# The same instructions of an attention and expert kernel, listed in another order

## The chip, the cores and the metric

One core of a Trainium2 chip runs the whole program. The metric is the device time in microseconds (us) of one execution, the median of three. The engines are PE (TensorE), DVE (VectorE), ACT (ScalarE), POOL (GpSimd) and SP (SyncE); SP computes nothing here and issues nearly all DMA transfers, one after the other.

## What is computed

Four batches of 12,608 tokens with 128 channels go through attention over 49 agents, and then 128 tokens of each batch, those with the largest score, through a small expert network.

```python
scale = 1.0 / np.sqrt(q.shape[-1])
agent_v = sm(agents, k) @ v          # softmax over the tokens, per agent
x = sm(q, agents) @ agent_v          # softmax over the agents, per token
scores = x @ w_gate
top_idx = argpartition(-scores[b], capacity)[:capacity]      # capacity 128
ye = relu(x[b, top_idx] @ w1) @ w2                           # 128 -> 1024 -> 128
out[b, top_idx] = x[b, top_idx] + sigmoid(scores[b, top_idx])[:, None] * ye
```

## The kernel before

Each batch's tokens are cut into seven blocks, six of 15 tokens for each of 128 partitions and one of 9 (`CHUNKS`). A block of q, k or v is one DMA of 960 KB (968 with v's column of ones), or 576 KB for the short one, into one of the eight tiles of the ring `in` (N_IN = 8). Results go out in blocks of the same sizes from tiles of the same ring. So a tile of `in` holds a load until PE has read it, or results from the first eviction into it until the store has landed.

The stages of a batch are these. **Keys** (`keys`, `scores`): PE multiplies a block of k with the agents (line 339, eight matmul records in the profile for each of two halves), DVE transposes the products into a tile (345) and takes their maximum (352); when all seven blocks are in, the maximum over the batch is spread over the partitions (369 to 384, `mb`). **Values** (`values`): POOL subtracts the maximum (394), ACT takes the exponential (397), and PE multiplies with the block of v (409). All blocks of a batch add up in the one bank `v`. `values_end` scales the result into the weights `ws` (425 to 466). **Queries** (`queries`): a block of q is multiplied and transposed like k; then the largest of each token (479, DVE), subtraction (481, POOL), exponential (483, ACT); for batch 0 alone the division too (485 to 490); a split into two halves of 16 bits (493 ACT, 494 POOL); a transposition on PE (509), copied out of PSUM by ACT or DVE (512). Queries need neither keys nor values, so their blocks may come early. **Gates** (533) and **rates** (547 to 561) give each token's score and divisor. **Results** (`results`): PE multiplies the transposed queries with `ws` (579), up to four tokens in a bank; DVE or ACT evicts the bank with the scaling (587 to 595) into an `in` tile, and SP stores it (600). **Choice and expert** (`topk`, `expert`): the 128 best of a batch (613 to 687), a gather by POOL (717), the network (725 to 831), a scatter by POOL (835) into the stored result, so after its stores.

The code records all this as some 1,300 operations with what they read and write, and then issues them in the order of a table of numbers, `ORDER`: each entry is an operation's number times two, plus one where the second of two allowed engines takes it (evictions and copies may go to DVE or ACT). Nothing else sets the order: `issue` goes through the table, gives each operation its tile from the ring (the one that became free first), and puts it at the end of its engine's queue. Every engine, SP included, works through its own queue in order; an instruction that has to wait holds up all that stand behind it on that engine.

```python
for code in order:
    i, way = code >> 1, code & 1
    engines, _, fn, bufs, after = self.ops[i]
    self._take(bufs)
    fn(engines[way])
```

The batches overlap: SP loads queries of batches 0 to 2 first, then keys of 0 and 1, and so on, as the table says. PSUM has six banks for scores, transpositions and results (ring `b`), one for the values and one for the gates.

Of the kernel before, what the change touches and what calls it, by code (L numbers as in the profile page):

```python
# [103 lines left out]
ORDER = (
    "0ca0cc0cg0ce0ci0t40t60ck0cm0co0cq0cs0cu0t80cw0cy0d00ns0nu0ny0ta0nw0o00tc0te0tg0ti0tk0tm0a20a80oo0ou0ow0aa"
    "0o20o40o60oq0os0a40qg0qm0qo0ts0tv0a60ac0ae0qi0pk0pm0to0pq0b60bc0b80po0qk0qq0ps0ag0o80ai0oa0qs0be0ba0tq0rc"
    "0ri0re0rk0bg0oy0bi0p008y0940oc0900og0pu0pw0rg09609209806q09a0ak0rm0am0oe0d20d40py0bk0oi06s06w06y06u07u0ro"
    "0ao00k15c08007w0bm0700bo0bq08207y00s00m07200u15i15e0rq09c0rs0ru0740p20p408400o15k0bs00q07600w15g09e15m05m"
    "0s00rw05o0d60bu0ry0d80s20p60qu09g0bw00y05q0100pc01201401605s05u0p80by0c101a07807a05w0aq0c20pe0q00pa0as01c"
    "01k0240ji02601e01m01o01i0180jq01g0c509i01q02i0060au0ay0js02a0ju01s01y0qw0b002802k02o02m02q01w02u01u02c022"  # L110
    "05y0q207c0aw07e08607g0qy15o15q0j40s802002e07i00e02g00i00g07m00800c0sa0q809k07o09m00a02w02y0300sc0se032034"
    "09o0880360qa02s07l08a0sg04u0021680iq16a0r00q40r416e16c0si06008c0iy0is16g0r316i0j215s15u03g03q08e0iu08g0sk"
    "03a0jw0380r609u0j609w0ko03k0ka0ic15w15z06206403i09q03c03e0iw0660j00q70kq0jy0k20ku0k40k80jk0ja09s0680kw0l0"
    "0j803m03o0jc0ky0jo0ks0jg0k60jm0je0ie0kc0ki0ik0ii0io0kg0km0l20ke0k00kk03u04404e04y04o18000003s0sm04a04004c"
    "08i0so0sq0sw04203w03y04604804g0ig0sy1600l408k16k16m04k08m08q0ss0l60l804m16o04w16208o0im08t0la0lm06a06c0n0"
    "04i04q04s0500521860540su0lc0lw16q05605818218418806e06i06k05a17417617817a17c05c06g0m60le05e05i05k05g14g14m"
    "14i19s19y19u14o1a014k0ma18w0lq0m00lg0fa0ea0fs0ed0lo0fu0fk0fm14q19w08w0e60b20b40e90fd16s0f60dy0f90e10c80e2"
    "0fg14s14u16u18a0ly0e50ee17e0041a207s06m06o09y0f20f40a007q0g218y1921940mg0mq0ms16w0dc0c608u0da1901960de0fy"
    "0g40gu0fj16y14w0m817g18c1a418e17i0n20mi14y17k1a617m0fo0li0lk0ls0lu0m20m40mk0mu0mc0me0mm0mo0mw0my1qg0n40n6"
    "0n80na0gw1060g00ey18g1540f00fr18i18k18m1560ze1ns11c0nc1080ne10a10c10e0ng0ni17s17u1qi18o1qm1qo0nk0no10i1nu"  # L120
    "1nw0nm1qk0fe0z01ny10g1o017o17q1a811e1qq18r0zm11k11m1501531980nq0gk0ra0go0pi0r81qs19a1qu0gn0ty0t20gg0zo11g"
    "0zq0gi11i0gr0z20z80z60za11o0z40zc10y0t011611010k0zs0do0g60s419c0dr0ds0dv0g910m0zg1181121o21o41o611a10o10q"
    "1000zi0zk1140zu1040zy0zw10s1m00gs10w0eo10211q0ga1m61m20tw0ok1m81m41l41241mw19e1o81oa0qc0pg11s0ek0er0hg11u"
    "11w1ma11y0gd0en0ge1aa10u0qe0om1ac0dg0es0s61oc0u00ho0hu0dj0ev12u12w1ae12k1l61la1lc0xi1l81n21n41my1oe1200hq"
    "0hs1220xm19g1ag1n019j0gy0he0y20h80xk0h00ha0hw1ai0y40uq12y12e12o13412a13o1mc1qw12m0hm12c1qy13e13q0yk0hk0yg"
    "1360u20y60h40xy0xw0xu13g0yi0hi0ya0yc13812612812g12i12q12s13013213a13c13i13s0fw0h60xq0us1n60y019k19n1le0h2"
    "0hc0uu0ye0ux1me0y80xo13k13m13u13w0um0up0xs0vm1r01r20vo13y0vy0eg0ei1400uy0w10v11gu1gg1g20v21420wc0wg0we0vu"
    "0dk0wj0vw0vq0vt1440w40w71go1461gq1gs1h21gw1r41480dn14a1h60vc0ve1r714c14e1lg1n81h01g40vg1gy0vj1mg1na1nc0wu"
    "0wm15a1700w818s1g60wa1h41g81660v80ew0dw1i01fo1h80w20wk1hm1pk0vb1gi1ga1mi0ww0hy19o1gm1gc0wp0i01gk0i21ge1li"
    "1ne1mo0ug1ak0u80ub0uj0i40i60wq17w1am18u0u41720i81580wy17y1640wt1mr0ia0u60uc19q1mk1ao0v41hg1ha0x11mm1lk1aq"  # L130
    "0v70uf1e61hk1hi1fw1hc1i21fq1i81fy1i61g01i41he1nk1dw0ym1ds1nn1ia1ic0yo1fs0yq1fu1hu1ho1hy1hs1dz1dv1lm1ls1lu"
    "1og1oo1ie1hq1hw1oi1pm1ig0ys1ea1ng1ii1ik1ni1pq1eo1im1ou1oq1po0yu1ow0yw1os1ps1pu1eg0yy1ee1eq1ei1e01e21ek1ec"
    "1e81oy1em1es1io1iq1c01bw1iy1j81is1j21jc1jm0vk1j01ji1f61eu1ew1ja1ey1jk1f01js1pw1k21kc1p01iu1iw1j41j61je1jg"
    "1jo1jq1f21f41c21c41c61be1by1f81fa1fc1fe1ci1bs1bm1fg1ca1jw1k61kg1ju1wm1wk1py1ck1k41p21p41ke1q01jy1k01k81ka"
    "1ki1kk1bp1bu1fi1bg1cc1q21fk1di1dl1km1fm1ko0x81as1q81ce0xb0x21we1e41c81wc0uk1kq1au1qb1ch1wo1p61q41b01q71b3"
    "1ks1ku1kw1l01l21cw1lo1cs1p81cy1ky1de1pc0xc1ra1ly1qe1no1pb0xe1pf1lr1dh1dm1ok1cm1wq1nq1om1d41ms1ws1cu1do1wu"
    "0x41pi1mu1qc1lw1pg1r81cp1ww0x61wy1d71x01x21s61da1d01uk1s21x41dd1rc1uu1uw1re1uy1s41x61s81sa1d31un1sd1vg1x8"
    "1to1ba1ry1v61v01vc1xc1bc1wi1cq1dq1wg0xg1d81tq1s01se1vw1vu1vq1vm1vs1xm1xo1vi1vk1xa1xe1xy1xi1xq1xl1y11xt1vo"
    "1tg1ya1tk1y21v41v21va1v81ve1ti1yd1y51tn1vy1w01w21bi1ts1tu1rg1w41y61u21ss1bl1tw1bq1rj1y91w61w81wa1rs1sk1sg"
    "1b41sv1yy1u41sm1aw1sj1ay1xu1b71ro1rq1so1sq1xx1ru1t21rk1ta1tc1ty1u61rn1u81yg1z01ua1t61u11z21t41z41z61uc1yk"  # L140
    "1sy1z81za1zc1ze1ug1uo1zg1xg1t91t11zi1ui1yi1ur1zm1zs1zw1zy1zk1b81rw1sw1ue1ye1yo1yq1zu1yu2021yw1te1us1ym1zo"
    "1zq2001ys204206"
)


# [904 lines left out]
```

## Time and profile before

| | |
|---|---|
| median of three runs | 295.34 us (294.12 to 296.73) |
| the profiled execution's own time | 295.63 us |
| its span, first to last instruction | 293.6 us |
| PE, DVE, ACT, POOL busy | 262.5, 224.1, 180.5, 143.2 us |
| moved by DMA | 106.67 MB |

Busy time is the time in which an engine has an instruction at work. Overlapping matmuls are counted once, so back-to-back work and work with small holes can look alike. "[3.46 <-DMA in<-kT]" behind an instruction means that its engine was idle for 3.46 us ahead of it and that the landing of a block of k ended the wait. A line of waits reads: engine, what it waited to do, what it waited for, us in total, how often, the longest.

### The profile page before, as it was taken

Reading aid. Unit: us, or ns where it says so; the run is one execution under the profiler, and the core shown is the slowest. Engines: PE = TensorE matmul, PEld = TensorE weight load, DVE = VectorE, ACT = ScalarE, POOL = GpSimd, SP = SyncE. Lnnn points to the kernel's source line nnn. Section 1 sums busy time; section 2 is a strip of 40 time slices with the busy share of each in tenths; the row PEclk is TensorE's granted clock in tenths of the full one; section 3 lists DMA queues with packets and bytes.
Section 4 is the critical chain, followed back from the end, with each engine's and each line's share of the span. In section 5 each row is a group of like instructions: output and inputs, shape, how many; then the busy total and the mean of one; then the engine's idle time right before and its main releaser. Section 6 shows DMA issues by size and latency. Waiting matters only on the chain.

```text
span 293.6 us, 8629 instructions
## 1 busy us (share of the span) xinstructions
PE 262.5 (89%) x3524; PEld 179.6 (61%) x3524; DVE 224.1 (76%) x516; ACT 180.5 (61%) x405; POOL 143.2 (49%) x110
## 2 busy tenths in 40 slices
PE   2897989899999999998999997798599999999990
PEld 1232334245497689845476896484358889968990
DVE  1598999999973893379977996697469858998740
ACT  1243896375554799144469979387337877899340
POOL 1457987979959697201649500532019951001022
PEclk9999999999999999999999999999789999999997
DMA  7999999999999979999998999998978996696991
GB/s 270 426 425 426 422 420 419 418 419 423 416 416 414 421 307 354 366 424 395 317 422 333 421 353 343 415 279 312 360 282 262 421 421 252 247 376 284 400 400 51
DMA packets 18587, 106.67 MB, mean 363 GB/s; under 512 B 2544, under 2 KB 3824, under 8 KB 18544
## 3 DMA queue, kind: packets, MB, share of 16 engines
q1 hardware_dynamic: 17760, 105.42, 91.2%
q8 instruction: 29, 0.48, 0.6%
q0 software_dynamic: 256, 0.52, 0.5%
q10 hardware_dynamic: 528, 0.13, 0.2%
q14 instruction: 14, 0.11, 0.1%
HBM read 79.85 MB, written 26.21 MB: 361 GB/s over the span
## 4 chain that ended last, share of the span: by engine, by line
PE 45%; DMA 30%; DVE 17%; ACT 4%; issue 2%; POOL 0%; POOLq 0%; SPq 0%; DVEq 0%; ACTq 0%
PE b L339 15%; PE v L409 12%; DMA in<-qT 12%; DMA out<-in 9%; PE b L579 8%; DMA in<-va 6%; DVE s L345 6%; PE b L509 5%; DVE mx L352 3%; DVE qm L479 3%; DMA in<-kT 3%; ACT in L595 2%; ACT ga L633 2%; DMA ag_sb<-agT 1%; PE x L533 1%
## 5 line engine op out<-in xcount | busy, mean ns | idle before, releaser
L339 PE MATMUL b<-in,ag_sb 128*32 128x480 f32 (+1 forms) x896 | 99.0, 567 | 19.0 <-DMA in<-kT 6.7
L345 DVE STREAM_TRANSPOSE s<-b 128x480 f32<-128x480 f32 (+1 forms) x112 | 67.7, 630 | 13.5 <-PE b L339 12.6
L339 PEld LDWEIGHTS b<-in,ag_sb 128*32 128x32 f32 x896 | 26.0, 112 | 64.4 <-issue 28.8
L394 POOL TENSOR_TENSOR s<-s,mb 128x735 f32<-128x735 f32 (+1 forms) x28 | 46.7, 1696 | 25.0 <-DVE mb L384 25.0
L579 PE MATMUL b<-ws,s 98*128 98x128 f16 x792 | 55.6, 219 | 1.6 <-DVE in L592 1.6
L512 ACT COPY s<-b 98x1024 f16<-98x1024 f16 (+2 forms) x36 | 32.3, 920 | 33.3 <-PE b L509 33.3
L494 POOL TENSOR_TENSOR f<-s,f 128x735 f16<-128x735 f32 (+1 forms) x28 | 41.1, 1475 | 23.5 <-ACT f L493 18.7
L579 PEld LDWEIGHTS <-s 98*128 98x128 f16 x792 | 47.8, 98 | 6.8 <-issue 5.5
L481 POOL TENSOR_TENSOR s<-s,qm 128x735 f32<-128x735 f32 (+1 forms) x28 | 38.1, 1369 | 26.2 <-DVE qm L479 18.0
L409 PE MATMUL v<-in,s 128*64 128x129 f32 x792 | 47.6, 274 | 1.7 <-DMA in<-va 1.7
L595 ACT ACTIVATE in<-b,r 128x128 f32<-128x128 f32 x149 | 40.9, 386 | 12.5 <-PE b L579 7.6
L409 PEld LDWEIGHTS v<-in,s 128*64 128x64 f32 x792 | 44.3, 136 | 4.1 <-DMA in<-va 1.2
L352 DVE TENSOR_REDUCE mx<-b 128x1 f32<-128x480 f32 (+1 forms) x56 | 32.9, 608 | 7.4 <-PE b L339 7.4
L509 PEld LDWEIGHTS <-f 128*98 128x98 f16 x396 | 25.5, 126 | 21.0 <-issue 14.6
L483 ACT ACTIVATE s<-s,lift 128x735 f32<-128x735 f32 (+1 forms) x28 | 24.4, 884 | 19.2 <-POOL s L481 19.1
L509 PE MATMUL b<-idh,f 128*98 128x128 f16 x396 | 30.7, 224 | 1.7 <-POOL f L494 1.4
L592 DVE TENSOR_TENSOR in<-b,r 128x512 f32<-128x512 f32 (+2 forms) x40 | 24.8, 645 | 5.1 <-DMA out<-in 3.2
L397 ACT ACTIVATE s<-s 128x735 f32<-128x735 f32 (+1 forms) x28 | 21.9, 790 | 5.4 <-POOL s L394 5.4
L628 DVE SCALAR_TENSOR_TENSOR ge<-b,top,minus 128x512 bf16<-128x512 f32 x32 | 23.9, 748 | 1.6 <-PE b L620 0.8
L479 DVE TENSOR_REDUCE qm<-s 128x15 f32<-128x735 f32 (+1 forms) x28 | 23.6, 856 | 0.2
L493 ACT CAST f<-s 128x735 f16<-128x735 f32 (+1 forms) x28 | 22.0, 788 | 2.8 <-POOL s L490 1.6
L633 ACT ACTIVATE ga<-b,top 128x512 bf16<-128x512 f32 x32 | 22.0, 689 | 0.8 <-PE b L620 0.3
(132 smaller groups left out, 227.4 us busy)
## 6 DMA issues: line engine op xcount, KB each, us to landing
in<-va SPq DMA_DIRECT2D x24, 967.5 KB, 8.0
in<-qT SPq DMA_DIRECT2D x24, 960.0 KB, 12.2
in<-kT SPq DMA_DIRECT2D x24, 960.0 KB, 9.8
out<-in SPq DMA_DIRECT2D x24, 960.0 KB, 8.1
in<-va SPq DMA_DIRECT2D x4, 580.5 KB, 8.8
in<-qT SPq DMA_DIRECT2D x4, 576.0 KB, 5.3
in<-kT SPq DMA_DIRECT2D x4, 576.0 KB, 9.9
out<-in SPq DMA_DIRECT2D x4, 576.0 KB, 6.6
```

The costliest lines, as they stand in the source:

```text
L339: nc.tensor.matmul(ps()[32 * i:32 * i + 32, :w], ag_sb[:, b, 32 * h:32 * h + 32], x()[:, w * i:w * i + w], start=True, stop=True,)
L345: nc.vector.transpose(s()[:, :n, 32 * h:32 * h + 32], ps()[:, :w].rearrange("p (t c) -> p t c", c=32))
L352: op("V", f"M{n}", lambda _, h=h, ps=ps: nc.vector.tensor_reduce(top[:, c, h:h + 1], ps()[:, :w], axis=AX.X, op=ALU.max), r=[ps], w=[(f"mx ...
L394: op("G", f"X{n}", lambda _, sv=sv, n=n: nc.gpsimd.tensor_tensor(sv(), sv(), d["mb"].unsqueeze(1).broadcast_to([P, n, A]), op=ALU.subtract ...
L409: nc.tensor.matmul(av()[o:o + AP_, :C + 1], s()[:, t], x3[:, t], start=(j < 2), stop=(j >= COLS - 2))
L479: op("V", f"qm{n}", lambda _: nc.vector.tensor_reduce(m, sv(), axis=AX.X, op=ALU.max), r=[s], w=[f"qm{b}{c}"])
L481: op("G", f"qx{n}", lambda _: nc.gpsimd.tensor_tensor(sv(), sv(), wide, op=ALU.subtract), r=[f"qm{b}{c}"], w=[s])
L494: op("G", f"ql{n}", lambda _: nc.gpsimd.tensor_tensor(f()[:, :n, A:], sv(), f()[:, :n, :A], op=ALU.subtract), r=[s, (f, 0)], w=[(f, 1)])
L509: nc.tensor.transpose(wide_pt()[:R, P * (t - lo):P * (t - lo) + P], f()[:, t, :], idh)
L512: (nc.vector.tensor_copy if e == "V" else nc.scalar.copy)(flat(ft()).bitcast(F16)[:R, P * lo:P * hi], wide_pt()[:R, :P * (hi - lo)])
L579: nc.tensor.matmul(p3()[:, t - lo], d["tile", c](t), ws[:, b, i, :C], start=(i == 0), stop=(i == 1))
L595: nc.scalar.activation(o4[:, t - lo], p3()[:, t - lo], AF.Copy, scale=d["r"][:, j0 + t:j0 + t + 1])
```

## The change

The table `ORDER` has other entries in the same number; the diff has nothing else. The new order was found with a charge on transfers that are issued late. One line of it stands for all:

```diff
@@ -102,44 +102,44 @@
 ORDER = (
-    "0ca0cc0cg0ce0ci0t40t60ck0cm0co0cq0cs0cu0t80cw0cy0d00ns0nu0ny0ta0nw0o00tc0te0tg0ti0tk0tm0a20a80oo0ou0ow0aa"
+    "0ca0cc0ce0cg0ci0ck0cm0co0cq16816a16c0cs16e16g0cu0cw0t40t616i16k16m16o0b60bc0be0b80ba0bg0bi17417617a1780bk"
...
```

Every engine's queue moves nearly everywhere. Two places of SP's queue are shown. "in_67" is one of the eight tiles in_64 to in_71; "out" is the result in memory; the last number is the columns of a block.

The first is the place of the first store, batch 0's second block. SP's queue before:

```order
L326 DMA in_70<-va 128x1935
L326 DMA in_69<-va 128x1935
L326 DMA in_71<-va 128x1935
L600 DMA out<-in_64 128x1920
L326 DMA in_65<-va 128x1935
L326 DMA in_71<-va 128x1935
L326 DMA in_70<-qT 128x1152
```

SP's queue after the change, at the same store:

```order
L326 DMA in_65<-va 128x1935
L326 DMA in_68<-va 128x1935
L600 DMA out<-in_70 128x1920
L326 DMA in_66<-qT 128x1920
L326 DMA in_67<-kT 128x1920
L326 DMA in_71<-kT 128x1920
L326 DMA in_68<-va 128x1935
L326 DMA in_70<-va 128x1935
```

The store was SP's 49th transfer and is now the 50th; the next load into the tile that it reads stands five rows behind it.

The second place is the keys of batch 3, among the stores of batches 0 and 1. SP's queue before:

```order
L600 DMA out<-in_65 128x1920
L600 DMA out<-in_70 128x1920
L600 DMA out<-in_66 128x1920
L326 DMA in_71<-kT 128x1152
L326 DMA in_70<-kT 128x1920
L326 DMA in_66<-kT 128x1920
L600 DMA out<-in_67 128x1920
L600 DMA out<-in_64 128x1920
L326 DMA in_67<-kT 128x1920
L326 DMA in_64<-qT 128x1920
L326 DMA in_70<-qT 128x1920
```

SP's queue after the change, with the last block of batch 0 (128x1152) and the keys of batch 3:

```order
L600 DMA out<-in_68 128x1152
L326 DMA in_67<-kT 128x1920
L326 DMA in_70<-kT 128x1920
L600 DMA out<-in_71 128x1920
L326 DMA in_66<-kT 128x1920
L326 DMA in_69<-kT 128x1920
L326 DMA in_64<-kT 128x1920
L326 DMA in_67<-kT 128x1152
L326 DMA in_70<-kT 128x1920
L600 DMA out<-in_65 128x1920
L600 DMA out<-in_68 128x1920
L326 DMA in_69<-qT 128x1920
```

Before, four loads here go into a tile that a store two or three rows ahead of them empties. After, none of the loads shown does; the tile in_68 is stored twice with no load into it between.

## Rows read from the trace of the kernel before

**Rows 1.** The page, part 1: busy us, share of the span, instructions.

```profile
PE 262.5 (89%) x3524; PEld 179.6 (61%) x3524; DVE 224.1 (76%) x516; ACT 180.5 (61%) x405; POOL 143.2 (49%) x110
```

**Rows 2.** The page, parts 2 and 3: all packets, and the queue that SP feeds.

```profile
DMA packets 18587, 106.67 MB, mean 363 GB/s; under 512 B 2544, under 2 KB 3824, under 8 KB 18544
q1 hardware_dynamic: 17760, 105.42, 91.2%
```

**Rows 3.** By stage: length; PE, PEld, DVE, ACT, POOL busy; clock, DMA share, GB/s.

```profile
10.00:100.00 90.00, 83.19 (x947) 40.05 (x940) 78.92 (x149) 51.41 (x73) 73.16 (x51) 1.00 1.02 420
100.00:115.00 15.00, 15.00 (x304) 13.46 (x303) 12.19 (x18) 13.88 (x21) 10.16 (x7) 1.00 0.87 333
115.00:240.00 125.00, 113.18 (x1628) 82.14 (x1625) 92.62 (x230) 80.28 (x194) 50.63 (x36) 0.97 0.95 360
287.00:293.60 6.60, 0.00 (x0) 0.00 (x0) 0.57 (x3) 0.00 (x0) 1.00 (x2) 0.78 0.10 35
208.00:216.00 8.00, 5.06 (x34) 2.27 (x38) 3.19 (x9) 2.33 (x8) 0.00 (x0) 0.57 0.97 353
5.16:115.00 109.84, 102.41 (x1275) 54.90 (x1277) 92.69 (x169) 65.73 (x94) 84.26 (x59) 1.00 1.00 409
```

**Rows 4.** Waits of the SP queue, 94 to 240 us: total, times, longest.

```profile
SPq L326 <- DMA out<-in: 36.7, 7, 9.2
...
SPq L600 <- ACT in L589: 15.3, 2, 13.1
```

**Rows 5.** Timeline of SP's issues, 94 to 110 us: start, length, issue.

```profile
94.14 0.33 SPq L326 DMA_DIRECT2D in<-va  x1
107.62 0.35 SPq L600 DMA_DIRECT2D out<-in  x1
```

**Rows 6.** Timeline of SP's issues, 174 to 230 us.

```profile
193.28 0.86 SPq L600 DMA_DIRECT2D out<-in  x2
203.41 0.34 SPq L326 DMA_DIRECT2D in<-kT  x1
...
225.51 2.97 SPq L326 DMA_DIRECT2D in<-va  x3
```

**Rows 7.** Waits of PE, 115 to 240 us, the three longest groups.

```profile
PE b L339 <- DMA in<-kT: 6.7, 3, 3.5
PE v L409 <- DMA in<-va: 1.7, 5, 0.4
PE b L579 <- DVE in L592: 1.6, 1, 1.6
```

**Rows 8.** DMA issues at 94 and at 203 us: size, us to landing.

```profile
in<-va SPq DMA_DIRECT2D x1, 967.5 KB, 13.6
in<-kT SPq DMA_DIRECT2D x1, 960.0 KB, 7.4
```

**Rows 9.** Timeline of PE, 200 to 222 us.

```profile
210.94 3.43 PE L339 MATMUL b<-in,ag_sb 128*32 128x480 f32 x16 [3.46 <-DMA in<-kT]
...
215.80 1.01 PE L339 MATMUL b<-in,ag_sb 128*32 128x480 f32 x8
...
218.80 2.63 PE L339 MATMUL b<-in,ag_sb 128*32 128x480 f32 x24
```

**Rows 10.** Timeline of PE at 71 us and from 105 to 122 us.

```profile
71.34 3.59 PE L339 MATMUL b<-in,ag_sb 128*32 128x288 f32 x40
...
106.09 0.61 PE L579 MATMUL b<-ws,s 98*128 98x128 f16 x8
...
110.47 10.13 PE L409 MATMUL v<-in,s 128*64 128x129 f32 x180
```

**Rows 11.** The page, part 5: line, count, busy, mean ns, idle before it.

```profile
L394 POOL TENSOR_TENSOR s<-s,mb 128x735 f32<-128x735 f32 (+1 forms) x28 | 46.7, 1696 | 25.0 <-DVE mb L384 25.0
L397 ACT ACTIVATE s<-s 128x735 f32<-128x735 f32 (+1 forms) x28 | 21.9, 790 | 5.4 <-POOL s L394 5.4
```

**Rows 12.** Waits of ACT for a store to land, 100 to 290 us.

```profile
ACT in L595 <- DMA out<-in: 4.9, 1, 4.9
```

More of the change, by code (lines that the diff above doesn't have):

```diff
@@ L104 @@
 ORDER = (
-    "0ca0cc0cg0ce0ci0t40t60ck0cm0co0cq0cs0cu0t80cw0cy0d00ns0nu0ny0ta0nw0o00tc0te0tg0ti0tk0tm0a20a80oo0ou0ow0aa"
[L106 to L139, printed above, removed]
@@ L140 @@
-    "1b41sv1yy1u41sm1aw1sj1ay1xu1b71ro1rq1so1sq1xx1ru1t21rk1ta1tc1ty1u61rn1u81yg1z01ua1t61u11z21t41z41z61uc1yk"
-    "1sy1z81za1zc1ze1ug1uo1zg1xg1t91t11zi1ui1yi1ur1zm1zs1zw1zy1zk1b81rw1sw1ue1ye1yo1yq1zu1yu2021yw1te1us1ym1zo"
-    "1zq2001ys204206"
+    "0ca0cc0ce0cg0ci0ck0cm0co0cq16816a16c0cs16e16g0cu0cw0t40t616i16k16m16o0b60bc0be0b80ba0bg0bi17417617a1780bk"
+    "0bm17c16q14g14m0ta14i14k14o17e17g14q0oo0oq0ou14s14u0ow0ns0nu0ny0os0tc0nw0oy0p008y0900940920o00960980pk0pm"
+    "14w14y0p20p409a0p60qg17i0bo0pq16w0qi0o20po0ps0t80bq0te0o40tg0qk07u16s08009c08209e0pu16u09g0bs0pw0p80o616y"
@@ new lines @@
+    "0py0q00a207w07y0a40a60840a80pc0qm0aa0860pf0pa08801c01k01o01e0q205m0qo01m01g08a05s0bu0q80qa08c0qq05u0q417k"
+    "0q606q06s06w0ac08e06y0bw17m15406u05o00y1500c201005q17o15615201i09i05w0060080by01407001208g08i0ti17q0c40o8"
+    "01q00a00e0c100c00i01s01u01w17s00g0ae09k0qs0qu17u02400k02i02c0160260ag0oa0og0oi09m0rc0ji0ka0ic02e00m00s028"
+    "02a01a02g01807208k02q0oc0oe08q09o05y08m00w08o0740qw0qy00u00o00q02u01y02k02202o02w09u02y02s02m0re0r00tk030"
+    "08s0r40iq0020j402003209q03409t0r70cy09w0600620r20tm0rg0ai0to0ri0tq0ik0ki0ts04u03g0d00tu0760km0jq0iy0ie078"
@@ new lines @@
+    "0ak04w0360rk0kk03q04004k03i0380640420io0am0ao0aq0js0ii07a0ig0jc0kc0kg03a0jg0ju0j00ke03k03u0ko0jw03c03e03s"
+    "0j60je0ja0j203m0d203o0jk0is0im0kq03w03y0k404404e04o04y0000ks07c0iu0jm0j80jo0k60ku0kw0k80jy07e07g04a04c066"
+    "0k20rm0l00iw0680d60d80d404m0as0ro0rq0rs0ru0l204604804g04i07i07k04q0l407m04s0500521pk0l60ky0l80540la05607o"
+    "0k00580lc0lg1pq1pm0rw05a15c19s1l41mw0le0li0lk0ry05c05e05g05i0ga0gd0g60g91po0ea0e20e50g20dy0s00s31ps0e019u"
+    "0g506a1pu0lm05k0lw0ly07s0e608w0da19y0e819w1a01l61la1lc0ec0n00mq1pw0lo15e1a215g15i15k15m0m61a406c0mg1a60m8"
@@ new lines @@
+    "1my1801861821n20s80sa1n01l81n41881840se0m00lq0eg0ej0ek0eo09y1n615o0ms1py1a818a18c1le1lg1aa06i0sg0fy0g006l"
+    "0sc0em0eq0ls0lu0m20m41ag08u1ac06e06h0au0aw0si07q0ay0ee18w10y0b018y1920es0sk0eu1101161941901af0z00z20z40z6"
+    "1960z80zc11a1180ma0fk0c60fs0b206m0b40za0fu1li1q01q21981n81ai0n20mi1121140mk0mu0n40sm0so0sq15q0mc0me0mm0mo"
+    "0mw0my0n60n819a19c18e0fm0na0ey11c0ge1060zs0ze0nc0fa19e0f00fc0ne0fg19k0c80f60fj06o19m0sw0f20ng0fo0dc0040f9"
+    "19g0a00f50fr0sz0ni0de10e10i10g15s19i0nk0no11k11e0ss11o0nm1001080zu0su11g10411m10211i10c0zm0zq0zg0zi0zo10k"
@@ new lines @@
+    "15u0nq0tw10s10w0gu10a10u0zk10m0qc0t01600t215w15y0s60om0go0ok0do0ra0r80hg0dr0zy0zw10q11q10o0gr11s0pi0pg0qe"
+    "0s40ty0ds11u0hw16211w0dg0hs0dj18g0gg0dk11y0gj0dn1na12012a12k0hk0ho1220hq12c0fw0ew1oo1m00fe12412e12o0u01oq"
+    "1m61m80du1os0xi1ou1m21q81qb1ow0xm0gk0xu0xq1m40gy0y412612812g12i12y13813i0gm13s12u13e13o18i0hm12w0u212m12q"
+    "0hu12s13q0yk0yc0hi0yg13g1340xs0xw0xy0ha0y20h41oy0vc0h20hc13618o0v81p01nc1p20ya0vb0ye0y818q0yi0y61ne0gw1ma"
+    "0h81mc0he0ve0y00h60h00xo13013213a13c13k13m13u13w13y1qg0gs1h81fo0dw1hm1gu18k18m1400vg0vj1420w80v40wa0v70wc"
@@ new lines @@
+    "1440hy1q414614814a1q61qi1qm1hg1ha0i01lk14c1qk0we1qo1hk1hi0i21fq1fw1lm14e1hc1he1fs1ng0i418u1am0uu1581lo1ni"
+    "1fu0ux1fy1lr0w41ak0uq0wg0uy15a0w70wj0i60us1g00i81ls19o0v11lu1qq0ia1ho1hu1gw1h21gg1i01g21hs1hy0xk1hq1hw1h0"
+    "1h41gy1h61nk0wu18s0um0wx1qs1qu1nm0up1me1qw1p41p61go1i81i21gi1ga1g41gq1i61ia1gm1gs1i41gk1ic1g81g61ge1ie0vk"
+    "0wk1ns0v21j21is1jc1640vq0wm0uc1700vt0wp1qy1gc0wy17w0vy1661720w11ig17y1ii19q0u80ym1ik0ua1im0uf1p81pc1r00vu"
+    "0yo1mg0x01r21pa1nu1ny0yq1ao1io1iy1js1ji1j80vw1e61pf1nw0wq1e80ws1ce0vm0ys0vo1o01es1iq1j00ug0ui1ea1b01d01f2"
@@ new lines @@
+    "1ju1f81jk1ja1jm1jw1iu1iw1j41j61je1jg1jo1jq1jy1k01we1k61kg0w20x21o21em1eg1ec1ek1eq1ee1ei0yu1eu1f41aq1ew1ey"
+    "1f61eo1b21f01d31o41mi1kc1ke1k21k41wk1cg1r40yw0yy1fa1fc1cw1d41mk1fe1fg1fi1cy1o61o81d61mm1k81ka1ki1kk1fk1ci"
+    "1km1r71ko1fm1oa1wm1cl1bi1as0x80u41kq1bl1au0u60xb1oc1ks1ku1oe1wo1kw1l01l21bw1mo1cs1ca1da1mr1by1ky1cc1cu1bs"
+    "1dd1lw1ms1di1dm1bv1do1cm1bm1co1wq1ws1bp1de1dg1r81og1oj1dk0xc1ly1wu1qc1ww0xf1wy1x01pi1ba1b41no1bc1c41c71mu"
+    "0x41aw1ra1ay1qe1pg1ok1om1nq0x71x21b71wg0uk1wc1d81cq1dq1be1bh1rc1uu1tk1tg1x41c01to1ts1x61c21uy1rs1re1tr1tn"
@@ L143 @@
+    "1ti1tu1rv1vg1ro1x81rg1rk1vc1ve1rq1v41dw1xc1ri1rm1dy1xa1xe1y61xu1xm1vi1vu1vo1vw1vq1vs1vk1vm1y91xo1y21y41xy"
+    "1e01xq1xw1e31xt1ta1ua1v01v81v21v61va1b81c80xg1tw1bq1wi1rw1vy1ds1uw1w01uc1y01w21tc1dv1xi1w41u21u61t21u51w6"
+    "1w81wa1t41ya1sg1ty1xg1xl1ye1si1yy1yc1u91u01ug1t61sk1sn1t91ui1so1sy1t01yk1sr1ss1yg1z01uo1s21z21z41z61sv1z8"
+    "1s41za1zc1uk1uq1um1yi1ze1sa1s61zg1zi1zm1ry1yo1s01zs1zw1zk1sd1s91e41ue1te1sw1us1se1zv1ym1zz2021ys1yu1zo1zq"
+    "2001yq1yw204206"
 )
```

## The prediction

> **What bounds the kernel now.** I read the page's busy times first [rows 1], then the transfers [rows 2], then the busy times by stage [rows 3], the waits and the timeline of the SP queue [rows 4 to 6], and the waits of TensorE last [rows 7]. All are of one execution of 293.6 us span, 295.63 us by its own clock, 0.1% above the median of 295.34 us.
>
> PE is busy 262.5 of 293.6 us and the queue that SP feeds holds the 16 DMA engines for 91.2% of the span, so two resources are nearly full, and neither is full all the time. From 10 to 100 us the queue moves 420 GB/s [rows 3]. At that rate a block of 960 KB (983,040 bytes) takes 2.34 us, and all 106.67 MB [rows 2] take 254 us. From 100 to 115 us it moves only 333 GB/s, and from 115 to 240 us 360 GB/s [rows 3]; against 420 that is (1 - 333/420) x 15 = 3.1 us and (1 - 360/420) x 125 = 17.9 us of missing transfer. From 240 us on mostly stores are left, which come as PE makes results, so there the queue waits for PE.
>
> Why the queue runs short is in SP's own waits. SP is in order, and a DMA that it can't issue yet holds all behind it. Loads and results share the 8 tiles of the ring "in". Seven loads wait until a store has landed, 36.7 us in all, 9.2 at most, and one store waits 13.1 us for its results [rows 4]. In the timeline [rows 5] SP issues a load at 94.14, then nothing until the store at 107.62; the loads issued until then are used up by about 107.7 (94.14 plus its 13.6 us to landing [rows 8]). At 193.28 two stores go out, the next load only at 203.41, when the first of them has landed [rows 6]; that load needs 7.4 us to land [rows 8], where a block in a full queue costs 2.34.
>
> PE then waits for what came late. From 115 to 240 us it is busy 113.2 of 125 us, idle 11.8 [rows 3]; nine waits make 10.0 of these, 8.4 of it for loads (kT 6.7, va 1.7), 1.6 for an eviction [rows 7]. Around the longest of them the granted clock is at half: its mean over 208 to 216 us is 0.57 [rows 3], so of these 8 us about 6.9 are at 1.2 instead of 2.4 GHz ((1 - 0.57) / 0.5 x 8). 16 score matmul records take 3.43 us there, 24 at the full clock 2.63 [rows 9]. From its first matmul at 5.16 us to 115 us PE is idle 7.4 of 109.8 us [rows 3], at a full queue up to 100 us: that start is set by the transfers and by VectorE, which has to turn and reduce each block. After PE's last matmul at 287.0 us 6.6 us of last store and scatter follow [rows 3].
>
> **The change, part by part.** No instruction is added or taken away; the same operations are listed in another order, with some evictions and copies given to the other of VectorE and ScalarE. So each part is a place in SP's order and what waits there.
>
> *Stores that a load waits for.* Before, the seven loads stand 2 or 3 rows behind the store whose tile they take (in_67 after 2, in_64 after 2, in_70 and in_66 after 3 in the rows shown of the change). One or two blocks stand between, 2.3 to 4.7 us of transfer; but SP issues the load only at the landing, and a load on a nearly empty queue took 7.4 us. After, only six loads take a tile from a store, 4, 4, 4, 5, 6 and 6 rows behind it. Three to five blocks stand between, 7.0 to 11.7 us of queue, more than the 5.1 (7.4 - 2.3) that a load needs ahead of its data. These waits should still be in the list of SP's waits, short, and cost the queue nothing.
>
> *The first store.* Before, 48 loads stand ahead of it, after, 49: 2.3 us more in the queue. PE's list up to the last product of that block had 544 score, 198 value, 221 transpose and 58 result records, now 504, 228, 198 and 52. At 40 score records in 3.59 us, 180 value records in 10.13 and 8 result records in 0.61, a transpose taken like a result record [rows 10], that is -3.6 + 1.7 - 1.8 - 0.5 = -4.2 us. So it is ready some 4 us earlier, and the queue's stock ends 2.3 us later: the 13.1 us wait should about halve and no longer reach the point at which the queue is empty. The 3.1 us of transfer missing there come back.
>
> *The later stores.* Counted from 0, the other six stores of batch 0 stand at 58, 63, 64, 67, 76 and 79 of SP's order instead of 57, 63, 67, 74, 79 and 80. Each waits for its results and blocks the loads behind it while it does. I price that at nothing, covered by what was issued ahead of it (in a full queue a load lands 13.6 us after its issue [rows 8], so some five blocks stand in it); without that cover each would cost what the first store did, 3.1 us.
>
> *The sum on PE.* PE has the same matmuls, so it ends earlier by what it no longer waits. Idle from 115 to 240 us: 11.8, of which I leave 1.0, since loads and PE now run at nearly the same pace; -10.8. The slow clock comes with the longest wait and should go with it: two score groups take 3.43 instead of 1.75 us [rows 9], so at least 1.7, and 6.9 us at half cost at most 3.4; I take -2.2. A stop also costs a restart: 8 score records alone take 1.01 us, in a row 0.72 [rows 9, 10], so 0 to 0.3 for each of nine, 0 to 2.7; I take -2.0. The start: of 7.4 us idle at most all and at least nothing can go; the queue is full there, and the first eight loads hold two of batch 0, whose normalising is VectorE's extra work, instead of three; between the ends I take -2.0. At the end the last store is 960 KB instead of 576: +0.9. Together 295.6 - 10.8 - 2.2 - 2.0 - 2.0 + 0.9 = **279.5, say 279 us**. The most that can go is 7.4 + 11.8 + 3.4 + 2.7 = 25.3, which with the 0.9 gives 271.2; that is the low end, 271. The queue alone, 254 us and the 6.6 of the end, would allow 261.
>
> *A rule against it.* The queue sustains 420 GB/s for 90 us [rows 3] while the mean over the span is 363 [rows 2]. The Trainium skill, "SBUF — State Buffer", section "Summary: rules for kernel authors", says to reckon about 358 GB/s for transfers between HBM and SBUF; by that rule 106.67 MB would take 298 us, the kernel would already stand at the limit and no order could help. The rows of 10 to 100 us contradict it.
>
> **The rivals.**
> *Half of it only.* The loads come in time, but other things behind them do not. After the batch's maximum each block goes through POOL (1.70 us) and ACT (0.79 us) [rows 11] before its value products; POOL is busy 84.3 of the first 110 us [rows 3]. Where PE's list brings a value product early, PE waits for that chain, 1.7 + 0.8 and up to 1.7 more for what POOL has in hand, about 4 us a time. For: POOL's waits for that maximum are 25.0 us, so the chain is serial [rows 11]. Against: PE waits for POOL in none of the nine [rows 7]. Two such stops and their restarts give 8.6 us back: 288.
>
> *No change.* SP's order has as many stores as before, and a store that is early in it blocks. If the queue runs dry at the new places as it did at the old, the 21 us of missing transfer stay: 293 to 298. For: SP waits for evictions as it is, 15.3 us for two of them [rows 4], which distance between a store and a load does not touch. Against: the first store's results come earlier against the queue. A cap on the mean rate, at the 363 GB/s of the span, would end here too: 106.67 MB are then 294 us of span, 296 by its clock. The 420 GB/s of 90 us speak against it; I give it 0.02 of the 0.1. The rule of the Trainium skill above would be such a cap.
>
> *Slower.* Loads further ahead hold tiles that results need. The 576 KB store of in_68 now stands behind the eight loads of batch 2's values and q; the next results go into in_68 too, with no load between, so their first eviction waits for that landing, and PE's products behind it fill the six banks of PSUM and stop. Before, the longest such wait was 4.9 us [rows 12]. The point is a PE that runs more than about 2 us ahead of the queue there; at worst it waits for the eight blocks, six of 2.34 and two of 1.4 us, 17 us in all; at one of the four places of this kind that makes 296, with 3 us more at another 299. Against: PE now has little lead, since both keep pace.
>
> **How the numbers follow.** Forecast, 271 to 284 us: 0.62. Half: 0.2, 284 to 292. No change: 0.1. Slower: 0.08, 298 to 310. About 1% is what a measurement of this kernel can tell from no change. Under 292.4 lie the first two: faster 0.82; same 0.1; slower 0.08. The range 271 to 291 leaves out the last two.
>
> **What would show it.** SP's loads wait for stores less than 15 us in all instead of 36.7. The slices from 100 to 210 us move over 400 GB/s; the last load of va goes out near 212 us, not 228 [rows 6]. PE waits for kT, va and qT less than 3 us after 115 us, its clock stays whole, it ends near 271, not 287. I am wrong if PE's idle time stays and the releaser's name has changed to POOL, ACT or DVE (half), if the slices around the stores still show 310 GB/s (no change), or if evictions wait for "DMA out<-in" by more than 15 us (slower).

## The result

The changed kernel takes 279.69 us (median of four executions, 279.43 to 281.55), the kernel before 295.58 us beside it (294.12 to 296.73): a ratio of 0.948, 95% interval 0.942 to 0.954. Forecast were 279.0 us in a range of 271 to 291. The profiled execution took 279.76 us with a span of 277.4 us, against 295.63 and 293.6. Ratios here and below leave disturbed executions out, so that they are not exactly the quotient of two medians.

The page of the changed kernel, busy times and transfers, which answers to [rows 1, 2]:

```profile
PE 256.9 (93%) x3524; PEld 178.4 (64%) x3524; DVE 221.6 (80%) x517; ACT 179.4 (65%) x394; POOL 143.3 (52%) x110
DMA packets 18588, 106.68 MB, mean 385 GB/s; under 512 B 2544, under 2 KB 3824, under 8 KB 18544
```

By stage, as [rows 3] (length; PE, PEld, DVE, ACT, POOL busy; clock, DMA share, GB/s), with the stretch from 100 to 210 us, in which the loads and the stores of batches 0 and 1 share the queue, and the end behind PE's last matmul:

```profile
10.00:100.00 90.00, 82.65 (x961) 41.84 (x958) 74.67 (x141) 55.04 (x79) 71.43 (x50) 1.00 1.02 421
100.00:115.00 15.00, 15.00 (x214) 8.95 (x213) 14.97 (x25) 5.15 (x8) 12.52 (x10) 1.00 1.01 395
115.00:240.00 125.00, 124.14 (x2011) 99.94 (x2006) 107.47 (x276) 95.63 (x236) 52.74 (x39) 1.00 0.99 395
100.00:210.00 110.00, 109.14 (x1670) 79.30 (x1669) 97.40 (x224) 76.22 (x166) 55.61 (x40) 1.00 1.01 414
208.00:216.00 8.00, 8.00 (x147) 7.89 (x146) 7.32 (x22) 7.83 (x22) 7.85 (x6) 1.00 0.91 307
270.86:277.36 6.50, 0.00 (x0) 0.00 (x0) 0.57 (x3) 0.00 (x0) 1.61 (x2) 0.79 0.14 43
```

Up to 100 us the sums hardly differ: PE 82.65 and 83.19 us busy, 421 and 420 GB/s. Then the queue goes on at nearly its full rate, 395 GB/s where it had 333 and 360, and PE is idle 0.9 us of the 125 from 115 us on, where it was idle 11.8. The granted clock is whole at 208 to 216 us (0.57 before).

Waits of PE from 115 to 240 us, the whole list, and of the SP queue from 94 to 240 us (total, times, longest), as [rows 7] and [rows 4]:

```profile
PE b L426 <- ACT ga L633: 0.9, 1, 0.9
```

```profile
SPq L326 <- PE b L339: 36.0, 19, 5.4
SPq L326 <- PE v L409: 28.4, 13, 4.3
SPq L600 <- DVE in L592: 22.1, 7, 12.0
SPq L326 <- DMA out<-in: 15.3, 4, 6.5
```

PE waits for no load any more. SP waits about as long as before, 121 and 124 us of these 146 over all groups, but 65 us of it, not 47, is for PE to free a tile, with transfers in the queue meanwhile, and 15.3 us, not 36.7, for a store to land. The longest wait of a store for its results, 12.0 us, stands behind the last load, where only weights wait with it; up to 210 us stores wait 11.0 us for results, before 23.9.

### The profile page after: what moved, and what is told of

Its sections match the earlier page's. It is cut to its first block, busy times and chain, and to the rows that moved or that the text cites. A ratio compares the mean times of both kernels' runs of the same rounds, so it can differ in the third digit from the quotient of the medians.

```text
span 277.4 us, 8607 instructions
## 1 busy us (share of the span) xinstructions
PE 256.9 (93%) x3524; PEld 178.4 (64%) x3524; DVE 221.6 (80%) x517; ACT 179.4 (65%) x394; POOL 143.3 (52%) x110
## 3 DMA queue, kind: packets, MB, share of 16 engines
q1 hardware_dynamic: 17760, 105.42, 93.5%
## 4 chain that ended last, share of the span: by engine, by line
PE 66%; ACT 13%; DVE 10%; POOL 3%; DMA 3%; issue 2%; POOLq 0%; DVEq 0%; ACTq 0%; SPq 0%
PE b L339 23%; PE b L579 14%; PE v L409 13%; PE b L509 7%; ACT ga L633 6%; DVE s L345 4%; PE x L533 3%; DVE qm L479 3%; ACT s L397 2%; PE b L827 2%; DMA ag_sb<-agT 2%; DMA out<-in 2%; POOL s L481 1%; ACT in L595 1%; ACT s L483 1%
## 5 line engine op out<-in xcount | busy, mean ns | idle before, releaser
L339 PE MATMUL b<-in,ag_sb 128*32 128x480 f32 (+1 forms) x896 | 95.0, 554 | 11.6 <-DMA ag_sb<-agT 5.2
L339 PEld LDWEIGHTS b<-in,ag_sb 128*32 128x32 f32 x896 | 25.4, 110 | 58.4 <-issue 23.0
L579 PE MATMUL b<-ws,s 98*128 98x128 f16 x792 | 54.9, 219 | 0.0
L512 ACT COPY s<-b 98x1024 f16<-98x1024 f16 (+2 forms) x41 | 36.9, 919 | 20.3 <-PE b L509 20.1
L409 PE MATMUL v<-in,s 128*64 128x129 f32 x792 | 47.3, 274 | 0.1
L595 ACT ACTIVATE in<-b,r 128x128 f32<-128x128 f32 x136 | 37.5, 388 | 8.2 <-PE b L579 7.8
L509 PEld LDWEIGHTS <-f 128*98 128x98 f16 x396 | 24.8, 124 | 17.4 <-issue 10.7
L592 DVE TENSOR_TENSOR in<-b,r 128x512 f32<-128x512 f32 (+2 forms) x43 | 26.9, 649 | 3.0 <-PE b L579 1.6
L628 DVE SCALAR_TENSOR_TENSOR ge<-b,top,minus 128x512 bf16<-128x512 f32 x32 | 23.9, 747 | 0.9
```

Source lines behind the costliest of these rows:

```text
L339: nc.tensor.matmul(ps()[32 * i:32 * i + 32, :w], ag_sb[:, b, 32 * h:32 * h + 32], x()[:, w * i:w * i + w], start=True, stop=True,)
L409: nc.tensor.matmul(av()[o:o + AP_, :C + 1], s()[:, t], x3[:, t], start=(j < 2), stop=(j >= COLS - 2))
L509: nc.tensor.transpose(wide_pt()[:R, P * (t - lo):P * (t - lo) + P], f()[:, t, :], idh)
L512: (nc.vector.tensor_copy if e == "V" else nc.scalar.copy)(flat(ft()).bitcast(F16)[:R, P * lo:P * hi], wide_pt()[:R, :P * (hi - lo)])
L579: nc.tensor.matmul(p3()[:, t - lo], d["tile", c](t), ws[:, b, i, :C], start=(i == 0), stop=(i == 1))
L595: nc.scalar.activation(o4[:, t - lo], p3()[:, t - lo], AF.Copy, scale=d["r"][:, j0 + t:j0 + t + 1])
```

## The experiments

The runs in one table: median, the median of the kernel before on the same chip, the ratio with its interval, and from the profiled execution PE's busy time and the rate from 100 to 210 us. A name such as k3.2 is block 2 of batch 3's keys, S0.4 the store of batch 0's block 4; SP's rows are counted from 0.

| kernel | us | before | ratio | PE busy | GB/s, 100 to 210 us |
|---|---|---|---|---|---|
| before | 295.6 | | | 262.5 | 361 |
| changed | 279.7 | 295.6 | 0.948 (0.942 to 0.954) | 256.9 | 414 |
| SP alone, rows 43 to 93 | 286.4 | 294.5 | 0.978 (0.968 to 0.988) | 258.4 | 390 |
| of these 43 to 53 | 295.5 | 294.5 | 1.005 (0.999 to 1.011) | 263.1 | 361 |
| 57 to 74 | 290.4 | 294.5 | 0.989 (0.984 to 0.994) | 261.7 | 374 |
| 75 to 93 | 289.8 | 294.5 | 0.986 (0.981 to 0.992) | 261.2 | 382 |
| changed, six stores two rows later | 288.0 | 295.2 | 0.979 (0.974 to 0.983) | 262.6 | 377 |
| three rows later | 296.3 | 295.2 | 1.004 (1.000 to 1.008) | 267.8 | 362 |
| nine stores one row earlier | 291.9 | 295.2 | 0.999 (0.991 to 1.007) | 259.3 | 378 |
| before, engine choices of the change | 307.3 | 295.2 | 1.043 (1.033 to 1.053) | 271.2 | 344 |
| changed, engine choices of before | 308.0 | 295.9 | 1.044 (1.035 to 1.054) | 267.1 | 391 |
| rearranged again, first | 293.3 | 295.9 | 0.989 (0.982 to 0.996) | 270.5 | 364 |
| second | 294.6 | 295.9 | 0.996 (0.992 to 0.999) | 270.8 | 380 |
| with fewer changes on PE | 280.8 | 294.8 | 0.957 (0.948 to 0.965) | 256.1 | 413 |

What is read from a trace belongs to the profiled execution's own time. It lies within 2 us of the median but for rows 43 to 53 (292.3 us), rows 57 to 74 (292.5), two rows later (292.4), three rows later (299.2) and nine stores earlier (289.7).

### SP's queue alone, and in three parts

The old order of the other engines, with SP's rows 43 to 93 permuted; the three parts are made one at a time in three further kernels.

```diff
 rows 43 to 53
-v1.3 q2.5 v1.1 v1.2 v1.0 S0.1 v1.4 v1.5 q3.6 v1.6 k2.3
+q2.5 v1.1 v1.2 v1.0 v1.4 S0.1 v1.3 v1.5 v1.6 k2.3 q3.6
 rows 57 to 74
-S0.3 k2.0 k2.5 k2.4 k2.2 q3.1 S0.6 q3.0 v2.0 q3.2 S0.5 v2.3 v2.1 v2.2 v2.4 v2.5 v2.6 S0.4
+k2.0 S0.4 k2.5 k2.4 k2.2 q3.1 S0.3 q3.0 q3.2 S0.5 v2.0 v2.3 v2.1 v2.2 v2.4 S0.6 v2.5 v2.6
 rows 75 to 93
-k3.3 k3.2 k3.1 S1.1 S0.2 S0.0 k3.6 k3.0 k3.4 S1.3 S1.4 k3.5 q3.5 q3.4 v3.0 v3.1 v3.2 v3.3 S1.2
+k3.3 k3.2 k3.1 S0.2 S1.1 S1.3 S0.0 k3.4 S1.4 k3.0 k3.6 k3.5 q3.5 S1.2 q3.4 v3.0 v3.1 v3.2 v3.3
```

All of it:

> Before, with PE, DVE, ACT and POOL in their old order and with their old choice of engine; only SP's rows 43 to 93 are permuted (counted from 0). Loads then stand 3 to 5 rows behind the store whose tile they take, where they stood 2 or 3, and the first store's data are asked for after one more load. Theory (SP's queue alone runs dry, the order of the other engines matters little): PE's waits for kT and va after 115 us go, the half clock goes, 278 to 285 us, so two thirds or more of the 16 us. Rival (the new order and engine choices of PE, DVE and ACT bring the gain, SP only follows): 292 to 297 us, as before.

The parts:

> Of that, only SP's rows 43 to 53: the first store goes out one row and the value loads around it are swapped. Theory as predicted (each gap in the transfers is paid by PE in the end): the 3.1 us of missing transfer at 107 us come back in part, 292 to 295 us. Rival a (that gap is the main cause): 288 us or less. Rival b (later gaps swallow it: what is not moved here is waited for at the next landing): 295 to 297 us, no change.

> Only SP's rows 57 to 74: three loads that stood 2 rows behind a store (36.7 us list: waits of 6 to 9 us) stand 3 rows behind or take another tile. Theory: two of the queue's gaps go, PE's first wait for va and part of its waits for kT go, 286 to 291 us. Rival (all gaps are made up for or lost again at the last pairs near 193 us): 294 to 297 us.

> Only SP's rows 75 to 93: the loads of batch 3's keys stand 3 to 5 rows behind their stores, not 2 or 3. Theory: the wait of 9.2 us at 193 us and the two behind it go, the granted clock stays whole at 208 to 216 us, 286 to 291 us. If the parts add up, the gains of this run, of rows 57 to 74 and of rows 43 to 53 sum to that of rows 43 to 93. Rival (PE is already too late by 190 us, the late pairs cost nothing of their own): 294 to 297 us.

All together gave 286.4 us, by the ratio 2.2% less than before, where the change took 5.2%: some two fifths of its gain (a quarter to three fifths by the interval), less than I expected of it and outside the rival's 292 to 297. The parts add up: by their ratios 0.5% more, 1.1 and 1.4% less make -2.0%. The second and the third part came out in the 286 to 291 us that the theory gave them, and in the third the granted clock is whole at 208 to 216 us (1.00). In the kernel with all parts, waits of the SP queue from 94 to 210 us:

```profile
SPq L326 <- DMA out<-in: 17.1, 5, 5.9
SPq L600 <- ACT in L589: 11.3, 2, 7.6
SPq L600 <- DVE rs L431: 7.1, 1, 7.1
```

and of PE from 100 to 285 us:

```profile
PE b L339 <- DMA in<-kT: 2.2, 3, 1.2
PE v L409 <- DMA in<-va: 1.0, 2, 0.8
```

The waits for stores have more than halved and PE waits 3.2 us for k and v, not 8.4. But up to 210 us stores still wait 27.4 us for results, 11.0 in the changed kernel, and the rate is 390 GB/s, not 414. SP's order alone did not make results come earlier; the order of the other engines is what is left for it. So the first rival, that only that order counts, has fallen, and so has my theory that it matters little. No run has the new order on the other engines and the old one on SP, so what that order brings alone is not shown.

The first part brought nothing, and its timeline says why. SP's issues in that kernel, 85 to 125 us (start, length, issue):

```profile
89.32 10.75 SPq L326 DMA_DIRECT2D in<-va  x4
107.75 0.35 SPq L600 DMA_DIRECT2D out<-in  x1
108.64 5.19 SPq L326 DMA_DIRECT2D in<-va  x3
```

One more value load stands ahead of the store, but it goes out only at the end of the first group, at 99.7 us, and the three behind the store are spread over 108.6 to 113.8 us: each waits until PE has read a tile. The rate from 100 to 115 us is 333 GB/s as before. With the old order on PE the tiles weren't there, whichever row the store had. What this gap would cost by itself remains open, since the edit did not close it.

### The distance, in the changed order

Only SP's rows of stores move, in the changed kernel; no other engine's order does. Six stores (S0.1, S0.5, S0.4, S0.2, S0.3, S1.1) two rows later, then three rows later; two of the places, by two rows:

```diff
-S0.5 k2.3 k2.2 k2.1 k2.4
+k2.3 k2.2 S0.5 k2.1 k2.4
-S1.1 v3.1 v3.0 v3.2 v3.3
+v3.1 v3.0 S1.1 v3.2 v3.3
```

> The changed order, with six stores put two rows later in SP's queue, so that the loads into their tiles stand 2 to 4 rows behind them, not 4 to 6; the other engines' queues are as in the changed kernel. Theory: a load that is issued at the landing of a store needs 7.4 us and finds (distance - 1) blocks of 2.33 us ahead of it, so the queue loses 7.4 - 2.33 x distance: 2.7 us at distance 2, 0.4 at 3. Three loads at 2 and one at 3: up to 8.5 us, PE has about 2 us of slack: 284 to 289 us. Rival (the gain sits in the other engines' order, distances are a by-product): 279 to 281 us.

> The same six stores three rows later: three loads at distance 1, two at distance 2, one at 4. By the same count 3 x 5.1 + 2 x 2.7 = 20.7 us are lost at most: 290 to 300 us, at or above the kernel before. Rival (distances are a by-product): 279 to 282 us.

Measured 288.0 and 296.3 us: 8.3 and 16.6 us more than the changed kernel. Two rows of six stores cost half of the gain, three rows all of it, and both lie where the count of missing transfer (8.5 and 20.7 us at most) put them; in the first two loads stand at 3, not one, which makes it 8.9. Waits of SP's loads for stores, 94 to 240 us, of the first kernel and then of the second:

```profile
SPq L326 <- DMA out<-in: 39.3, 6, 11.4
```

```profile
SPq L326 <- DMA out<-in: 42.6, 5, 12.9
```

The second one's busy times and rate from 130 to 150 us:

```profile
130.00:150.00 20.00, 16.98 (x241) 10.39 (x238) 13.47 (x35) 6.70 (x12) 2.27 (x3) 0.94 0.84 330
```

In the changed kernel itself these 20 us have 424 GB/s and PE busy throughout. The sum of these waits is no measure of the loss: the execution with 39.3 us took 292.4 us and the one before, with 36.7, took 295.6; an order further below waits 30.3 us for landings and takes 280.5, where the changed kernel waits 15.3 and takes 279.8.

The other direction: nine stores (S0.0, S1.2 and S1.4 too) one row earlier. Two of the places:

```diff
-k2.6 S0.5 k2.3 k2.2 k2.1 k2.4 S0.4 S0.2 q3.4
+S0.5 k2.6 k2.3 k2.2 k2.1 S0.4 S0.2 k2.4 q3.4
-k3.2 k3.6 k3.1 S1.2 S1.4 q3.3 S1.1 v3.1
+k3.2 k3.6 S1.2 S1.4 k3.1 S1.1 q3.3 v3.1
```

> The changed order, with nine stores put one row earlier in SP's queue: the loads stand 5 to 7 rows behind, but SP reaches each store earlier and waits longer for its results, with the next loads held behind. As predicted (a store's wait is covered by what was issued ahead of it): 279 to 281 us. Rival (the changed order stands at the edge, a store that waits one block longer empties the queue): 283 to 288 us. If distance were all that counts: 276 to 279 us.

Measured 291.9 us, 12 more than the changed kernel, worse than every guess. Waits for stores have nearly gone, and the time has gone up. SP's waits from 94 to 240 us, its issues from 123 to 146 us, and PE's two longest stops behind 100 us:

```profile
SPq L600 <- ACT in L595: 13.0, 2, 7.1
SPq L600 <- ACT in L589: 5.6, 1, 5.6
SPq L326 <- DMA out<-in: 4.2, 3, 1.9
```

```profile
125.23 7.22 SPq L326 DMA_DIRECT2D in<-kT  x4
138.10 0.82 SPq L600 DMA_DIRECT2D out<-in  x2
139.01 0.85 SPq L326 DMA_DIRECT2D in<-kT  x1
```

```profile
113.68 3.52 PE L409 MATMUL v<-in,s 128*64 128x129 f32 x60 [1.57 <-DMA in<-va]
149.06 3.29 PE L339 MATMUL b<-in,ag_sb 128*32 128x480 f32 x16 [4.11 <-DMA in<-kT]
```

SP waits 5.6 us for the results of S0.4, until 138.10, with k2.4 queued behind; that load goes out at 139.01, right behind the two stores; its tile was free, since S0.5, which empties it, had landed at 133.5. PE stops 4.1 us for it, and then its 16 score records take 3.29 us instead of 1.82, at a mean granted clock of 0.54 from 149.0 to 152.4 us. At the first store it is the same on a smaller scale: v1.1 goes out at 104.99 instead of 102.98 us, and PE waits 1.6 us for it. In the changed kernel k2.4 is the last of the four loads ahead of the stores, and PE does not stop for it:

```profile
127.02 6.67 SPq L326 DMA_DIRECT2D in<-kT  x4
136.30 0.82 SPq L600 DMA_DIRECT2D out<-in  x2
```

```profile
143.09 1.82 PE L339 MATMUL b<-in,ag_sb 128*32 128x480 f32 x16
```

Compared matmul by matmul, PE is 1.6 us later than in the changed kernel behind the first place, 5.7 us more behind k2.4, and 2.9 us more in all the rest. S1.4 and S1.1 wait for their results too, 6 and 7 us, but PE idles only 1.1 us ahead of the products of k3.1, the load behind S1.4. PE's first long stop in the two kernels with later stores is for the same block k2.4 (2.6 and 3.0 us): there it goes out when S0.5 has landed, at 140.0 and 142.1 us, in the changed kernel at 133.4.

So a store's row has two sides. Later, and the load into its tile comes late; earlier, and all loads behind it do. The changed order stands between the two: one row earlier, or two later, at a few places takes half of the gain or more.

### The engine choices

The 75 evictions and copies that the change gives to the other engine, put into the order of before, and those of before put into the changed order. One of the 75 entries, the copy of a transposition (L512) that ACT did and DVE does, in the order of before:

```diff
-0s2
+0s3
```

> Before's order on every engine, SP's included; only the 75 evictions and copies that the change gives to the other of VectorE and ScalarE are given to it here too. Theory (the choice of engine fits the place of an operation in its order and brings nothing by itself): no gain, 294 us or slower, up to 303. Rival (the change gains by a better split of evictions between VectorE and ScalarE): 280 to 290 us.

> The changed order on every engine, but the 75 evictions and copies are given to VectorE or ScalarE as they were before. Theory (a choice of engine fits its own order; in a foreign one an engine is loaded twice in a stretch, results come late, stores and with them loads are held up): slower than the changed kernel by 8 to 25 us, 288 to 305. Rival (the choices are free, the order of loads and stores is all): 279 to 283 us. Together with the same change in the kernel before, which cost 12 us, it shows whether the choices are worth anything alone.

Measured 307.3 and 308.0 us. Neither choice is worth anything in the other's order: 12 us lost in the first, 28 in the second, both above the ranges that I gave (up to 303 and 305). In the second the stretch to look at has 391 GB/s, more than the kernel before; among PE's waits those for single results of ACT and DVE are long (5 to 300 us):

```profile
PE b L805 <- ACT ga L633: 4.3, 1, 4.3
...
PE b L620 <- ACT in L589: 2.1, 1, 2.1
PE b L640 <- DVE ge L628: 2.1, 1, 2.1
```

PE is also busy 10.2 us longer than in the changed kernel, at a mean granted clock of 0.975 instead of 0.995. Matmul by matmul it is 5 us late before the first store, 16 at 240 us and 27 at the end, so late stores, the path that I had named, are not the whole of it; the rest is not taken apart. That a better split between VectorE and ScalarE brought the gain is out; that the split has to fit the order is shown.

### Rearranged again

Two orders that I made from the changed one, all engines, with durations from the traces; and a third, in which a change of operation on PE has its price.

```
entries that left their place:  PE  DVE  ACT  POOL  SP
first                          264  255  139    46  42
second                         277  264  142    47  35
third                          197  236  126    46  27
```

> The changed order rearranged once more, on all engines, with durations from the rows of the two traces (a block 2.33 us, 7 us from a late load's issue to its landing, the instructions at their mean times); six loads stand 3 to 6 rows behind a store. Theory (PE still loses some 7 us to small waits between 10 and 180 us, half of them behind single evictions and transpositions, and the queue's cover stays as it is): 272 to 277 us. Rival (the changed order sits at a narrow place, any move empties the queue, as one row more or less did): 281 to 292 us.

> A second rearrangement of the same kind, from another random start, with loads 4 or 5 rows behind their stores. The same theory: 272 to 277 us; the same rival: 281 to 292 us. Two such orders that agree speak for the durations that they were made with, two that differ by over 5 us for chance.

> The changed order rearranged on all engines as in the two orders before, but each change of operation on PE (a score group behind a value product, and so on) is counted at what the rows show: eight score matmuls take 0.94 us behind another operation and 0.81 in a row, a value product of seven 0.98 and 0.79. PE's queue changes its operation 193 times, the changed kernel's 240, the two orders before 300 and 288; loads stand 3 to 5 rows behind a store. Theory (the two orders before lost their time in these changes: PE busy 270.5 us for the same matmuls where the changed kernel is busy 256.9): PE busy 245 to 254 us and 268 to 277 us in all. Rival (something else than the changes made PE's work longer there, or the order of the loads loses its cover when all is moved): 282 to 295 us.

The first two took 293.3 and 294.6 us, outside what the theory gave, and above the rival's range too. They agree to 1.3 us, which speaks against chance. Their PE is not idle where it counts (139.96 of 140 us busy from 100 to 240 us in the first) and yet late: it is busy 13.6 us longer than the changed kernel's with the same matmuls. Scores and value products by line, busy time and mean of one record, first kernel; then the third:

```profile
L339 PE MATMUL b<-in,ag_sb 128*32 128x480 f32 (+1 forms) x896 | 103.3, 571 | 13.6 <-DMA in<-qT 6.1 <-DMA ag_sb<-agT 6.0 <-DVE s L345 1.1
...
L409 PE MATMUL v<-in,s 128*64 128x129 f32 x792 | 51.2, 276 | 0.0
```

```profile
L339 PE MATMUL b<-in,ag_sb 128*32 128x480 f32 (+1 forms) x896 | 95.0, 559 | 11.7 <-DMA ag_sb<-agT 6.3 <-DMA in<-qT 1.9 <-DMA in<-kT 1.7
...
L409 PE MATMUL v<-in,s 128*64 128x129 f32 x792 | 47.7, 274 | 1.0 <-DMA in<-va 1.0
```

The changed kernel has 95.0 and 47.3 us in these lines. So 8.3 and 3.9 of the 13.6 us stand in two lines whose records are hardly longer (571 and 554 ns, 276 and 274): they overlap less. PE changes its operation 300 times in the first order and 240 times in the changed one, and 43 of the 60 more lead to a score group (29) or a value product (14). By their places in six of the traces, eight score records take 0.94 us behind another operation and 0.81 in a row, a value product of seven 0.98 and 0.79. At 0.13 and 0.19 us each the 43 make some 6 us, the other 17 some 1. The mean granted clock, 0.987 against 0.995, leaves 0.013 x 292.7 - 0.005 x 277.4 = 2.4 us of full-speed work missing. Some 4 us stay open; small waits for a bank that vanish in the overlap would look like this, and no run shows them.

With the changes priced, the third order takes 280.8 us, PE busy 256.1. Both lie above what the theory gave (268 to 277 and 245 to 254 us) and below the rival's 282. It is 12.5 us faster than the first, its busy time 14.4 us less, so as far as one order can tell the changes matter; that nothing else made the difference is not shown. But it is no faster than the changed kernel (the two intervals overlap), for all its 47 fewer changes: 38 of these lead to results and transpositions, which cost 0.03 to 0.08 us, and PE is idle 4.2 us after 115 us where the changed kernel's is idle 1.3. Its SP waits 30.3 us for stores and its rate from 100 to 210 us is 413 GB/s, which says once more that this wait alone is no measure. No order here beats the changed one.

## Why the prediction was right, and where not

**What bounds the kernel.** Right. Two resources nearly full that starve each other, and SP's queue between them. The rate from 100 to 210 us orders the kernels that differ in SP's queue alone: 361, 374, 382, 390 on the old compute order, 362, 377, 378, 414 on the new one, and the times fall with it (295.5, 290.4, 289.8, 286.4; 296.3, 288.0, 291.9, 279.7), but for 377 and 378. By the profiled executions' own times, to which the rates belong, these two fall into line (292.4 and 289.7 us), and 374 ties with the 361 of rows 43 to 53 (292.5 and 292.3). It is no cause by itself: in the first rearranged order it is 364 with PE busy all the time, and SP waits 84.5 us for PE to free a tile, 65 in the changed kernel.

**Stores that a load waits for.** Right in mechanism and size. The count put the two displaced kernels at 284 to 289 and 290 to 300 us; 288.0 and 296.3 came. "Less than 15 us in all" came out as 15.3, but was a poor sign: 4.2 us went with 291.9 us, 30.3 with 280.8.

**The first store.** The wait fell from 13.1 to 0.9 us (SP issues the store at 104.31), more than halved, and the stretch has 395 GB/s, so (395 - 333) / 420 x 15 = 2.2 of the 3.1 us came back. The reason that I gave was half of it. I read the gap as the store's wait; the run that moved the store one row and the value loads around it left the gap as it was (the store's wait fell to 7.6 us, the rate stayed at 333 GB/s), since the loads behind it had no tile either. By the trace it is closed because PE's new list reads tiles earlier (the loads behind the store go out from 107.0 us on); no run tests that by itself.

**The later stores, priced at nothing.** Right for the rows that they have, wrong as a judgement of how firm that is: I counted five blocks of cover, and one row earlier cost 12 us, of which 5.7 at one block behind S0.4 and 1.6 behind the first store.

**The sum.** Terms for the profiled executions, forecast and measured:

| term | forecast | measured |
|---|---|---|
| PE idle, 115 to 240 us | -10.8 | -11.0 (11.82 to 0.86) |
| slow clock and restarts (PE busy) | -2.2 - 2.0 | -5.6 (262.5 to 256.9) |
| start (PE idle to 115 us) | -2.0 | +0.2 (7.4 to 7.6) |
| behind PE's last matmul | +0.9 | -0.1 (6.6 to 6.5) |
| idle behind 240 us, and what lies outside the span | 0 | +0.6 |
| sum | -16.1 | -15.9 |

One step failed, the start. I let DVE's lesser work there count for 2 us; the waits of PE from 5 to 115 us in the changed kernel say that it is the queue, with 4.3 us for blocks of q where the kernel before had 4.2:

```profile
PE b L339 <- DMA ag_sb<-agT: 5.2, 1, 5.2
PE b L339 <- DMA in<-qT: 4.3, 7, 1.1
PE b L339 <- DVE s L345: 1.3, 2, 0.7
```

A block lands every 2.33 us and its 16 score records take 1.82, so PE can't keep up a lead there; [rows 3] had it already, with 420 GB/s in both. It was made good by PE's busy time, which fell by 1.4 us more than forecast: 4.0 of the 5.6 us are in the score line, 99.0 to 95.0, where the half clock and the stops were. At the end the last store is larger by 0.9 us but no longer stands behind another: 4.36 us from issue to landing, 6.59 before. The restarts were mis-sized in the working as well: the 40 score records in 3.59 us [rows 10] hold two groups of 288 columns, so that 0.72 us in a row is too short. Groups of 480 columns take 0.81, a restart is then 0.2 us and nine of them at most 1.8, not 2.7, less than the 2.0 that I took; the same 40 records made the first store's -3.6 us, which should be -4.0. So that the sum came within 0.3 us is luck, by misses of both signs: 2.2 us at the start and 0.6 in the rest against 1.4 in the busy time, 1.0 at the end and 0.2 in the idle time.

**The rivals.** Half of it only: POOL and ACT took no place of the waits that went. As a size it came true in the kernel with SP's rows alone (286.4), where stores waited for results. No change: the mean rate is 385 GB/s, above the 363 at which a cap on it would have held the time; the Trainium skill's 358 GB/s ("SBUF — State Buffer", section "Summary: rules for kernel authors") is not the limit here either, with 421 GB/s over 90 us and 414 over the next 110. Slower: no eviction waits for a store's landing after 100 us in the changed kernel, on ACT or DVE; the tile that is stored twice without a load between costs nothing.

**The signs.** The last load of va goes out at 211.2 us (forecast 212), PE's work ends at 270.9 (271), PE waits for loads 0 us after 115 (under 3), the clock is whole. From 100 to 210 us the mean is 414 GB/s (over 400), with single slices of 7 us at 371 to 396.
